# A boot stage rearranged: two products to GpSimd, the states' last sums to ScalarE, own scores ahead of the updates

## The chip, the cores and the metric

One core of a Trainium2 chip runs the whole kernel. The metric is device time in microseconds, as the median of several runs. The core has five engines with a queue each: TensorE (PE; its weight loads are PEld), VectorE (DVE), ScalarE (ACT), GpSimd (POOL) and SyncE (SP), which here only issues transfers. GpSimd does not read TensorE's result memory, PSUM, in this kernel; VectorE and ScalarE do.

## The reference

A recurrent attention block with a decaying state, and behind it a dense block with a shrinking activation:

```python
for t in range(S):                       # B, H, S, D = 4, 8, 768, 48
    cur = einsum('bhd,bhe->bhde', u * k[t], v[t])
    y[t] = einsum('bhd,bhde->bhe', r[t], state + cur)
    state = w[t][..., None] * state + einsum('bhd,bhe->bhde', k[t], v[t])
x = y as (B*S, H*D) = (3072, 384)
h = x @ w_in                             # 384 -> 2048
out = (h - tanh(h)) @ w_out              # 2048 -> 384
```

All in float32, with decays w between 0.80 and 0.95.

## The kernel before, in words

The sequence of each batch element is cut into two halves of 384 tokens, which makes eight blocks. The attention of a block is turned into matrix products over chunks of 64 tokens. Products of decays within each chunk come from scans on VectorE: `post` (from a token to the end of its chunk, method `behind`) and `pre` (from the chunk's start, divided by the chunk's whole decay, method `before`). `times_behind` multiplies k into `post`, `times_before` multiplies r into `pre`. Two sets of scores follow on TensorE: `own` (k·u with r, of which the diagonal is kept) and `earlier` (`post` with `pre`, of which what lies above the diagonal is kept). Masked copies on VectorE (`copy_predicated`) bring them into one tile, `scores`. The result of a block is the scores times v (`from_scores`) plus `pre` times the state at the start of each chunk (`from_states`).

While one block's dense products run on TensorE, the next block's attention is fitted in between them. The first block has nothing to hide behind: function `boot` does its attention alone, ahead of everything else, and this is the stage that the change touches. It handles the eight heads as four pairs, in two halves: `h1` is pairs 2 and 3, `h2` is pairs 0 and 1. For each half it runs, in this order of dependence: decays, `times_behind`, k times u on ScalarE (`times_u`), own scores, `post` transposed on TensorE (`turn_1`) and copied by ScalarE (`turn_2`), `times_before`, earlier scores, the products k·v for every chunk (`update_half`), and a scan over the chunks that turns them into states (`states_half`). `states_half` also returned one small sum for each pair, the state handed on to the next block. The results of a pair are copied from PSUM to the tiles `xT`, the input of the dense products (`result_out`). Pairs 0, 1 and 2 fill 96 of the 128 rows of xT[0], xT[1] and xT[2]; pair 3 goes to a tile `late`, from which six small transfers fill the holes, two for each xT tile (`fill_holes`).

At the same time the weights come in: sixteen tiles of 768 KB (`more_weights`, from SyncE's queue), each converted by three ScalarE instructions and one or two of VectorE (`convert`). There are five buffers for them. Six of the sixteen are issued in the boot; the second, third and fourth wait for a given matrix product on TensorE (`begin_behind`), those in the main loop for a ScalarE instruction.

The order on TensorE, VectorE, ScalarE and SyncE is the order in which the program is written, and each engine goes through its queue in order: an instruction that waits holds up all those behind it. Only GpSimd's order is left to the framework. Three PSUM tiles take turns in the boot (`scratch`), and the products k·v use two more (`pair`), which are later the first accumulators of the dense block.

## Time and profile before

| | us |
|---|---|
| median of 3 runs | 544.35 (544.01 to 544.61) |
| the profiled execution | 545.07 |
| its span, first to last instruction | 543.3 |
| PE busy | 534.1 (98%) |
| DVE busy | 459.0 (84%) |
| ACT busy | 403.7 (74%) |
| POOL busy | 6.5 (1%) |
| first dense product starts at | 23.50 |

Times in the trace count from the start of the span. A row of the timeline gives the start, the duration, the engine, the line of the kernel, the operation and its operands; the bracket tells how long the engine stood idle before it and what ended the wait. A row of the transfers gives the size of one and the time from its issue to its landing. The granted TensorE clock is 1.000 over the whole span.

### The profile page before, as it was taken

The page shows a single profiled execution, that of the slowest core. Times are in us where ns is not written, and L with a number is a line of the kernel's source. Part 1 is how long each engine was busy: PE and PEld are TensorE (multiplying, and loading weights), DVE is VectorE, ACT ScalarE, POOL GpSimd, SP SyncE. Part 2 cuts the span into 40 slices and gives each one's busy share as a digit, 9 for nine tenths or more (in the row PEclk, how much of TensorE's full clock was granted, in tenths as well). Part 3 has the DMA queues.
Part 4 walks back from the last instruction along what each step waited for, and adds up shares of the span by engine and source line. Part 5 has one row for each costly group of instructions (what it writes and reads, how often), then busy time and mean ns, then how long its engine had stood idle before and what let it go on. Part 6 is the DMA issues. An engine that isn't in the chain of part 4 may idle for free.

```text
span 543.3 us, 14866 instructions
## 1 busy us (share of the span) xinstructions
PE 534.1 (98%) x5682; PEld 403.3 (74%) x5682; DVE 459.0 (84%) x943; ACT 403.7 (74%) x814; POOL 6.5 (1%) x47
## 2 busy tenths in 40 slices
PE   7999999999999999999999999999999999999996
PEld 5756665678877777777887787877788788777874
DVE  7999999999989989798997979879797997557463
ACT  4899986888668876688767886688866885766561
POOL 1100000000000000000000000000000000000000
PEclk9999999999999999999999999999999999999999
DMA  7798732252311631154112532136321420100101
GB/s 276 234 402 311 259 119 74 97 137 63 122 42 54 162 118 57 43 147 119 60 56 87 122 103 70 48 97 151 84 89 46 122 27 3 56 1 0 45 1 46
DMA packets 53048, 56.34 MB, mean 104 GB/s; under 512 B 21488, under 2 KB 50928, under 8 KB 52976
## 3 DMA queue, kind: packets, MB, share of 16 engines
q1 hardware_dynamic: 52592, 55.18, 33.9%
q8 instruction: 48, 0.79, 0.6%
q14 instruction: 24, 0.20, 0.1%
q10 hardware_dynamic: 288, 0.10, 0.1%
q0 software_dynamic: 96, 0.07, 0.1%
HBM read 44.73 MB, written 4.72 MB: 91 GB/s over the span
## 4 chain that ended last, share of the span: by engine, by line
PE 88%; DVE 6%; ACT 2%; issue 2%; DMA 1%; SPq 0%; DVEq 0%
PE hp L871 41%; PE acc L999 27%; PE att L999 7%; PE att L757 4%; PE acc L950 3%; PE acc L977 2%; PE att L494 2%; PE att L575 1%; PE att L871 1%; ACT up L264 1%; DMA r<-in_rT 1%; DVE w_sb L268 1%; PE acc L871 1%; DVE scores L502 1%; DVE states L587 1%
## 5 line engine op out<-in xcount | busy, mean ns | idle before, releaser
L871 PE MATMUL hp<-xT,w_sb 128*128 128x384 f32 x738 | 259.3, 488 | 0.4 <-ACT h L876 0.4
L871 PEld LDWEIGHTS hp<-xT,w_sb 128*128 128x128 f32 x738 | 131.8, 190 | 70.0 <-ACT h L876 1.3
L999 PE MATMUL acc<-forms,g 128*128 128x128 f32 x954 | 133.2, 276 | 0.0
L876 ACT ACTIVATE h<-hp 128x384 f32<-128x384 f32 x123 | 60.3, 490 | 96.6 <-PE hp L871 96.5
L999 PEld LDWEIGHTS acc<-forms,g 128*128 128x128 f32 x954 | 122.0, 192 | 10.3
L879 DVE SCALAR_TENSOR_TENSOR h<-h,s 128x384 f32<-128x384 f32 x128 | 70.5, 551 | 51.9 <-ACT s L894 51.8
L920 DVE TENSOR_TENSOR g<-g 128x256 f32<-128x256 f32 x265 | 103.2, 418 | 7.4 <-PE acc L999 6.5
L895 ACT ACTIVATE qa<-s,shift 128x384 f32<-128x384 f32 x113 | 69.5, 615 | 3.7
L897 ACT ACTIVATE junk<-s,shift 128x384 bf16<-128x384 f32 x113 | 67.7, 599 | 0.0
L879 DVE SCALAR_TENSOR_TENSOR g<-qa,h 128x384 f32<-128x384 f32 x112 | 61.6, 550 | 1.6 <-ACT qa L905 0.2
L894 ACT ACTIVATE s<-h 128x384 f32<-128x384 f32 x113 | 59.2, 523 | 3.6
L999 PEld LDWEIGHTS acc<-w_sb,g 128*128 128x128 f32 x318 | 46.8, 191 | 9.7 <-ACT sums L967 0.3
L999 PE MATMUL acc<-w_sb,g 128*128 128x128 f32 x318 | 53.0, 276 | 0.0
L999 PE MATMUL att<-w_sb,g 128*128 128x128 f32 x212 | 35.5, 275 | 0.0
L999 PEld LDWEIGHTS att<-w_sb,g 128*128 128x128 f32 x212 | 31.1, 192 | 5.3
L1034 DVE TENSOR_TENSOR sums<-sums 128x256 f32<-128x256 f32 x84 | 32.8, 406 | 1.7 <-ACT sums L1011 1.4
L950 PE MATMUL acc<-w_sb,sums 128*128 128x384 f32 x96 | 33.9, 489 | 0.1
L264 ACT ACTIVATE up<-raw 128x768 f16<-128x768 f32 (+1 forms) x32 | 33.1, 1074 | 0.0
L950 PEld LDWEIGHTS acc<-w_sb,sums 128*128 128x128 f32 x96 | 17.9, 190 | 13.0 <-DVE sums L879 1.2
L417 DVE TENSOR_TENSOR_SCAN pre<-w,start 128x780 f32<-128x780 f32 x14 | 25.0, 1783 | 0.8
L429 DVE TENSOR_TENSOR_SCAN post<-w,seed 128x780 f32<-128x780 f32 x14 | 24.9, 1775 | 0.0
L897 ACT ACTIVATION_READ_ACCUMULATOR junk<-s,shift 128x1 f32 x113 | 21.1, 187 | 0.0
(118 smaller groups left out, 528.8 us busy)
## 6 DMA issues: line engine op xcount, KB each, us to landing
raw<-in_weights SPq DMA_DIRECT2D x16, 768.0 KB, 7.1
w<-in_wT SPq DMA_DIRECT2D x7, 780.0 KB, 4.7
k<-in_kT SPq DMA_DIRECT2D x7, 768.0 KB, 4.6
r<-in_rT SPq DMA_DIRECT2D x7, 768.0 KB, 4.6
v_sb<-in_v SPq DMA_DIRECT2D x8, 576.0 KB, 4.0
k<-in_tokens SPq DMA_DIRECT2D x7, 576.0 KB, 5.0
r<-in_tokens SPq DMA_DIRECT2D x7, 576.0 KB, 4.7
out_y<-sums SPq DMA_DIRECT2D x18, 128.0 KB, 1.8
```

The costliest lines, as they stand in the source:

```text
L264: return lambda: nc.scalar.activation(out=to, in_=of, func=AF.Copy, scale=scale, bias=bias)
L417: return nc.vector.tensor_tensor_scan(out=self.tile("pre")[:, cols], data0=self.tile("w")[:, cols], data1=start[:, 0:n * NCH * LP], initia ...
L871: nc.tensor.matmul(hp, lhsT=w_in_sb[:, f, kc, :], rhs=xT[kc], start=(kc == KC - 1), stop=(kc == 0))
L876: return h, nc.scalar.activation(out=h, in_=hp, func=AF.Copy, scale=1.0 / UPSCALE)
L879: return lambda: nc.vector.scalar_tensor_tensor(out=out, in0=in0, scalar=scalar, in1=in1, op0=op0, op1=ALU.mult)
L894: nc.scalar.activation(out=s, in_=h, func=AF.Square)
L895: nc.scalar.activation(out=qa, in_=s, func=AF.Square, bias=shift[:, 4:5])
L897: nc.scalar.activation(out=junk[:, 0:NB], in_=s, func=AF.Relu, bias=shift[:, 5:6], accum_out=excess[:, at:at + 1])
L920: return lambda: nc.vector.tensor_tensor(out=G[:, to:to + 2], in0=two(G, g_at(q, a0), g_at(q, a1)), in1=two(G, g_at(q, b0), g_at(q, b1)), ...
L950: nc.tensor.matmul(acc, lhsT=g[:, j * P:(j + 1) * P], rhs=w_out_sb[:, f, :], start=(f == self.first), stop=(f == NF - 1))
L999: nc.tensor.matmul(to, lhsT=G[:, g_at(q, a), :], rhs=rhs, start=start, stop=stop, skip_group_check=True)
L1034: ops.append(lambda op=op, at=at: nc.vector.tensor_tensor(out=at[0], in0=at[1], in1=at[2], op=OPS[op]))
```

## The change

`times_before` and `times_behind` can be given an engine, and for the second half both go to GpSimd; the second of them also moves up, ahead of VectorE's copy of the first half's scores. The small sums that followed the scans of the states are split. ScalarE copies one of their terms from PSUM into the next block's state tile (`last_half`, two copies for each half). One VectorE instruction for all four pairs adds the other term later, in the main loop (`onwards`, at step 3 of block 0). `earlier()` of the first half moves ahead of `turn_2` of the second. `from_states` no longer goes pair by pair in the boot. For the second half, own scores are computed ahead of `update_half`, and their masked copy stands ahead of the scans. The second weight load moves from behind the first `update_half` to behind the first `from_states`. The hole transfers of xT[2] and xT[1] all go to SyncE's queue and those of xT[0] to GpSimd's, where they alternated between the two. In the general path, which only runs for unusual decays, `together` copies by halves of rows.

```diff
+SPARE = 94
-        def times_before(self, p0, n):
+        def times_before(self, p0, n, engine=nc.vector):
             t = self.before_each(p0, n)
-            return nc.vector.tensor_tensor(...)
+            return engine.tensor_tensor(...)
-        def times_behind(self, p0, n):
+        def times_behind(self, p0, n, engine=nc.vector):
...
         def states_half(self, p0):
                 nc.vector.tensor_tensor_scan(out=to, data0=kv, data1=by, initial=0.0, op0=ALU.add, op1=ALU.mult)
-            return [lambda p=p0 + p, kv=kv: nc.vector.tensor_tensor(
-                out=states[1][:, p, 0, 0:D], in0=first_states[:, p, :, NCH - 1], in1=kv[:, :, 0], op=ALU.add)
-                for p, kv in enumerate(self.by_column)]
+        def last_half(self, p0):
+            for p, kv in enumerate(self.by_column):
+                nc.scalar.copy(out=states[1][:, p0 + p, 0, 0:D], in_=kv[:, :, 0])
+        def onwards(self, p0, n):
+            to = states[1][:, p0:p0 + n, 0, 0:D]
+            nc.vector.tensor_tensor(out=to, in0=first_states[:, p0:p0 + n, :, NCH - 1], in1=to, op=ALU.add)
...
-                      3: ("times_behind 2",),
+                      3: ("times_behind 2", "onwards"),
...
-        own = blk.own(ps, h1, spare=94, ahead=5, late=6)
+        own = blk.own(ps, h1, spare=SPARE, ahead=5, late=6)
         blk.turn_1(ps, h1)
         blk.times_before(h1, UP)
         earlier = blk.earlier(ps, h1)
         blk.behind(h2, UP)
         blk.take_whole(h2, UP)
+        blk.times_behind(h2, UP, nc.gpsimd)
         first_a, first_b = convert(*raws.pop(0), tiles=2)
         own()
         blk.turn_2(h1)
         blk.totals_by_column(h2)
         blk.update_half(pair, h1)
-        begin_behind(blk.done, more_weights(nc.sync))
-        blk.times_behind(h2, UP)
         blk.times_u(h2, UP)
         blk.turn_1(ps, h2)
+        earlier()
         blk.turn_2(h2)
-        earlier()
         blk.results(ps)
         blk.result("from_scores", both[0])
-        run(blk.states_half(h1))
-        blk.result("from_states", both[0], True, apart=True)
+        blk.states_half(h1)
+        blk.last_half(h1)
+        blk.result("from_states", both[0], True)
+        begin_behind(blk.done, more_weights(nc.sync))
         blk.before(h2, UP)
-        blk.update_half(pair, h2)
-        blk.times_before(h2, UP)
+        blk.times_before(h2, UP, nc.gpsimd)
         own = blk.own(ps, h2)
         own_scored = blk.done
+        blk.update_half(pair, h2)
         run(first_a[:1])
         blk.result_out((3,), [nc.scalar.copy] * 2)
         blk.result_out((2,))
         earlier = blk.earlier(ps, h2, ahead=1)
         scored = blk.done
-        onwards = blk.states_half(h2)
         own()
+        blk.states_half(h2)
         run(first_a[1:])
-        needed = 2 * KC - 2
-        blk.fill_holes([nc.sync, nc.gpsimd], range(needed, 2 * KC))
+        blk.last_half(h2)
+        blk.fill_holes(range(4, 6))
         begin_behind(own_scored, more_weights(nc.sync))
-        blk.fill_holes([nc.sync, nc.gpsimd], range(needed))
+        blk.fill_holes(range(2, 4))
+        blk.fill_holes(range(2), nc.gpsimd)
         begin_behind(scored, more_weights(nc.sync))
         later.load("w")
         second_a, second_b = convert(*raws.pop(0))
         third_a, third_b = convert(*raws.pop(0))
         run(second_a)
         more_weights(nc.sync)
         blk.results(ps)
         blk.yp.reverse()
-        blk.result("from_states", both[1], apart=True)
+        blk.result("from_states", both[1])
         earlier(1, 1)
         earlier(0, 1)
         for p in reversed(both[1]):
             blk.result("from_scores", (p,), True, more=True)
         later.load("k")
         more_weights(nc.sync)
-        run(onwards)
         run(first_b[:1])
         for p in reversed(both[1]):
             blk.result_out((p,), [nc.scalar.copy, nc.vector.tensor_copy])
```

More of the change, by code (lines that the diff above doesn't have):

```diff
@@ L769, in together, with fill_holes @@
                     stretch(of, cross)
-            self.result_out(ALL)
-            self.fill_holes([nc.sync])
-        def fill_holes(self, engines, which=range(2 * KC)):
+            self.result_out(ALL, None if spread else [nc.scalar.copy] * 2)
+            self.fill_holes()
+        def fill_holes(self, which=range(2 * KC), engine=nc.sync):
             for n in reversed(which):
@@ L776, in fill_holes @@
                 src = 64 * (n // KC) + 16 * (n % KC)
-                engines[n % len(engines)].dma_start(out=self.xT[i][64 * h + D:64 * h + 64],
-                                                    in_=self.late[src:src + 16, :])
+                engine.dma_start(out=self.xT[i][64 * h + D:64 * h + 64], in_=self.late[src:src + 16, :])
         def phase(self, ps, name):
@@ L1058, in plan @@
             phases = {6: ("turn",), 7: ("update",), 10: ("earlier",), 13: ("results",)}
-            before = {0: ("behind 2", "take_whole 2"), 2: ("behind 0", "take_whole 0"), 3: ("times_behind 2",),
+            before = {0: ("behind 2", "take_whole 2"), 2: ("behind 0", "take_whole 0"), 3: ("times_behind 2", "onwards"),
                       4: ("times_behind 0",), 5: ("before 2",), 6: ("before 0",), 7: ("times_before",),
```

6 lines of the change are left out of this document (3 added, 3 removed).

## The prediction

> **What bounds the kernel now.** I read the page first (TensorE is busy 98% of the span), then the windows of the trace by stage, because the change lies in the first 25 us only.
>
> ```profile
> 25.00:50.00 25.00, 24.62 (x84) 14.50 (x83) 22.76 (x42) 23.45 (x33) 0.00 (x0) 1.00 1.02 384
> 50.00:76.00 26.00, 26.00 (x247) 15.60 (x245) 25.35 (x48) 26.00 (x39) 0.13 (x2) 1.00 0.59 198
> 76.00:543.30 467.30, 462.24 (x4760) 357.37 (x4760) 390.18 (x819) 337.38 (x719) 2.21 (x25) 1.00 0.28 76
> ```
>
> The columns after the window's length are the busy times of PE, PEld, DVE, ACT and POOL, then the granted clock, the DMA engines' share and GB/s. From 76 us on TensorE alone is full, so a microsecond won or lost by then stays. Between 25 and 76 us three engines are full together, and the DMA engines up to 50 us: a gain at 25 us need not arrive at 76. Who leads there is told by the chain of waits, ScalarE's timeline, the issue of one weight load and the time from that issue to its landing.
>
> ```profile
> 50.47 0.56 DVE sums L879
> 76.10 2.20 PE acc L950 x6
> 36.59 0.92 ACT L264 ACTIVATE w_sb<-raw 128x768 f32<-128x768 f32 x1 [0.85 <-DMA raw<-in_weights]
> 22.81 0.69 SPq L251 DMA_DIRECT2D raw<-in_weights  x1
> raw<-in_weights SPq DMA_DIRECT2D x1, 768.0 KB, 13.8
> ```
>
> Back from 76.10 the chain is VectorE to 50.47, then ScalarE. ScalarE last stood idle at 36.59, 0.85 us for the sixth weight tile, which was issued at 22.81 and landed 13.8 us later, at 36.6. From there it works without a gap to 76 us. So the end follows the landing of these loads: a later landing goes through whole, while an earlier end of the boot would only lengthen the wait at 36.59.
>
> **The change part by part.** First the product k·decay of the second half, which GpSimd takes over and which stands earlier in the order.
>
> ```profile
> 3.88 0.68 SPq L369 DMA_DIRECT2D k<-in_kT  x1
> k<-in_kT SPq DMA_DIRECT2D x1, 384.0 KB, 8.4
> 12.36 0.96 DVE L443 TENSOR_TENSOR post<-k,post 128x768 f32<-128x768 f32 x1
> 0.82 0.20 POOL masks.py:197 MEMSET ident<- 128x128 f32 x1 [0.29 <-POOLq L1445]
> 0.96 0.75 POOL L171 MEMSET start<- 128x780 f32 x1
> 1.75 0.28 POOL masks.py:199 TENSOR_SCALAR_AFFINE_SELECT ident<-ident 128x128 f32<-128x128 f32 x1
> ```
>
> Its input k was issued at 3.88 and landed 8.4 us later, at 12.28. VectorE began at 12.36, so the earlier place cannot start it earlier: GpSimd begins at about 12.30. No row has a GpSimd product. From below it is 0.75 us, a write-only pass of 780 elements; from above 2.25 us, three such passes (two reads and a write that share nothing). The two MEMSETs give (0.75-0.20)/652 = 0.84 ns per element written and 0.09 us fixed; the select reads as well and takes 0.08 us more on 128 elements, 0.63 ns per element read. Two reads and a write of 768 elements: 768 x 2.10 + 0.09 = 1.70 us. This is the value I take. The product ends at 14.00, where VectorE's ended at 13.32.
>
> What waits for it is the transpose on TensorE, and its queue behind it.
>
> ```profile
> 10.35 0.88 PE L517 MATMUL att<-ident,post 128*128 128x128 f32 x6
> 11.16 0.93 PE L494 MATMUL att<-pre,post 48*64 48x64 f32 x48
> 13.38 0.87 PE L517 MATMUL att<-ident,post 128*128 128x128 f32 x6
> 14.31 0.90 PE L697 MATMUL att<-scores,v_sb 64*48 64x64 f32 x48
> 15.50 1.56 PE L679 MATMUL att<-pre,first_states 48*48 48x64 f32 x37 [0.28 <-PEq L717]
> 18.00 0.90 PE L494 MATMUL att<-r,k 48*64 48x64 f32 x48
> 13.24 1.02 DVE L502 COPY_PREDICATED scores<-mask_all,att 128x768 f32<-128x768 uint8 x1
> ```
>
> The transpose moves from 13.38 to 14.06 (+0.68). The products with the scores follow a transpose's start by 0.81 us (10.35 to 11.16): 14.87. VectorE no longer holds them, since its score copy of 13.24 now starts at 12.36, 0.88 earlier, and the scans behind it end before 15. The products with the states follow by 1.19 (14.31 to 15.50), drain included: 16.06. Without the split by pairs four places of the array alternate, as in the rows of 0.90 us; I take 0.90 for these 48 and end them at 16.96. The old form ran 15.50 to 17.16, so TensorE is by now 0.2 us ahead. Here begins the trouble: the second weight load, formerly behind the first half's update, now waits for this end.
>
> VectorE gains: the four small sums leave it (two of them in the way), and so does the product with r.
>
> ```profile
> 15.57 0.24 DVE L632 TENSOR_TENSOR states<-first_states,hp 128x48 f32<-128x48 f32 x1
> 17.95 0.96 DVE L436 TENSOR_TENSOR pre<-r,pre 128x768 f32<-128x768 f32 x1
> 18.83 0.75 DVE L631 TENSOR_TENSOR_SCAN first_states<-acc,first_totals 128x288 f32<-128x288 f32 x1
> 19.50 0.73 DVE L631 TENSOR_TENSOR_SCAN first_states<-hp,first_totals 128x288 f32<-128x288 f32 x1
> 16.82 0.25 PE L616 MATMUL acc<-v_sb,ks 64*64 64x48 f32 x1
> 22.68 0.89 PE L697 MATMUL att<-scores,v_sb 64*48 64x64 f32 x48 [0.24 <-DVE states L632]
> ```
>
> The input of the product with r, ready at 17.95 now, comes 0.88 and two sums (0.48) earlier, at 16.6, and GpSimd ends 1.70 later, at 18.3. TensorE does the own scores first, to 17.9 (16.96+0.90), then the update, to 19.0 (1.18, as from 16.82 to 18.00 now). Only then does it need that product, which is hidden with 0.7 us to spare, even at 2.25. Without this cover it would cost all it lasts beyond. VectorE's own scores are copied beside the update; its two scans (18.83 to 20.23, 1.40) follow it to 20.4, the states' products (0.90) to 21.3; the gap of 0.24 and the scores' products of 0.89 end at 22.4, where they now end at 23.57. That is about 1.15 us ahead on TensorE. The one sum for all pairs in the main loop, in place of the four, falls into a stretch in which VectorE was busy 22.76 of 25 us: nothing; without that room, 0.24 or a little more.
>
> ScalarE takes four copies. I price each like VectorE's 128x48 sum, 0.24.
>
> ```profile
> 15.18 0.91 ACT L264 ACTIVATE w_sb<-raw 128x768 f32<-128x768 f32 x1
> 16.62 0.97 ACT L729 COPY late<-att 48x384 f32<-48x384 f32 x2 [0.53 <-PE att L679]
> 17.99 2.01 ACT L264 ACTIVATE up<-raw 128x768 f16<-128x768 f32 x2
> 19.86 0.89 ACT L264 ACTIVATE w_sb<-raw 128x768 f32<-128x768 f32 x1
> 20.66 1.96 ACT L264 ACTIVATE up<-raw 128x768 f16<-128x768 f32 x2
> 23.29 0.84 ACT L729 COPY xT<-att 48x384 f32<-48x384 f32 x2 [0.67 <-PE att L697]
> 23.80 1.04 DVE L729 COPY xT<-att 48x384 f32<-48x384 f32 x2 [0.74 <-ACT xT L729]
> ```
>
> Its copy of the transposes moves with them, by 0.68. What followed at 15.18 so comes at 15.86: first two small copies (0.48), then the first conversion (0.91), to about 17.2. So the copies into the tile "late" go from 16.62 to 17.2 (+0.58), the next conversions from 17.99 to 18.57; these end at 20.58, and two more small copies at 21.0.
>
> SyncE's queue decides the rest.
>
> ```profile
> 18.12 0.64 SPq L777 DMA_DIRECT2D xT<-late  x1
> 18.95 0.41 SPq L251 DMA_DIRECT2D raw<-in_weights  x1
> 19.42 1.15 SPq L777 DMA_DIRECT2D xT<-late  x2
> raw<-in_weights SPq DMA_DIRECT2D x1, 768.0 KB, 4.3
> xT<-late SPq DMA_DIRECT2D x1, 24.0 KB, 4.5
> 25.21 0.30 PEld L871 LDWEIGHTS acc<-xT,w_sb 128*128 128x128 f32 x2 [0.50 <-DVE xT L729]
> ```
>
> The second load is issued at about 16.97, not at about 13.4 (its old trigger ends just before the transposes of 13.38), and lands 4.3 us later, at 21.27, where ScalarE has been ready since 21.0. Its three conversions take 2.76 (19.86 to 22.62) and end at 24.03, and ScalarE's halves of the last xT copies are queued behind them. VectorE's halves, which start 0.51 after ScalarE's (23.80 against 23.29), so start near 24.55 and end 1.04 later, at 25.6. So the 1.15 us on TensorE find no xT: the third part of the first dense product starts near 25.65, now 25.21.
>
> Both hole transfers for xT's last tile are now SyncE's; they start behind xT's copy, at 18.70 instead of 18.12, and take 0.64 and 0.58 (half of 1.15) to issue. The third load, free since 17.9, goes out at 19.9, not 18.95. The loads behind it follow in order, in a stream with no gap to catch up in: the sixth lands 0.95 us later, ScalarE waits for it until 37.5 and the chain passes it on. The holes of the second tile are queued behind the third load, at 20.3 and 20.9, and land 4.5 us later as their like did, at 25.4 at the latest of the two; this could make the 25.65 up to 0.4 more, still under 0.95. Those of the first tile go to GpSimd's queue behind its second product, 18.3, with seven microseconds to spare.
>
> **Sum.** 0.95 us on the profiled execution's 545.07 us (span 543.3) gives 546.0; that execution lies 0.72 above the median of 544.35, so on the median 545.3. With GpSimd at 0.75 the transposes are as early as now, and it is 0.0; at 2.25 it is 1.5. Small copies at 0.1 instead of 0.24 take off 0.3.
>
> **The rivals.** (a) Faster: the loads are early enough all the same, and TensorE's 1.15 us arrive: 543.2. It needs the second load down by 21.0 and the sixth no later than 1 us before 36.6. For it speaks that the old second load had its data 2.2 us before use (17.7 and 19.86); against it the wait of 0.85. It decides where the second load is issued before 16.6.
> (b) Slower: GpSimd is kept out while VectorE copies scores. Old scores, mask and PSUM data may amount to two reads of SBUF; then the copy of 12.36 to 13.38 holds the product until 13.40, 1.10 later, and 0.95 becomes 2.05: 546.4. No row shows both engines at work together on SBUF. The Trainium skill (SBUF — State Buffer, "Who interferes with whom") says that a VectorE instruction with two SBUF inputs shuts out a GpSimd instruction that reads SBUF for its whole length, and one with a single SBUF input does not; counted as mask and PSUM data, this copy has one, and by that rule the 0.95 stands.
> (c) It does nothing: the sixth load's landing hangs on the slowest DMA engine's backlog and not on the issue of the third, and the 0.44 at 25 us vanishes in ScalarE's wait: 544.4.
>
> **How the numbers follow.** About 0.2%, 1.09 us, is what a measurement can tell from no change here. The forecast has 0.60: its own range is 544.2 to 545.9, and somewhat less than half of it (0.27) lies above 545.44, because every unpriced wait adds; 0.33 lies within. Rival (a) 0.15, (b) 0.17, (c) 0.08. Faster 0.15, same 0.41, slower 0.44. The range from 543.2 to 546.8 takes in (a) and (b).
>
> **What would show it.** Right: GpSimd's first product starting at 12.3, not at 11.4, and lasting 1.4 to 2.0; the transposes near 14.06; the second load issued near 17.0; ScalarE idle before its conversion, with "DMA raw" as releaser; the third load issued near 19.9 and ScalarE's last wait ending near 37.5. Wrong: this wait ending at 36.6 or sooner, the first dense product starting before 23 with ScalarE's copies right behind, or a product of more than 2.5 us.

## The result, and the profile after

| | before | after |
|---|---|---|
| median, same chip (range) | 544.61 us (543.97 to 545.20) | 548.71 us (547.40 to 550.85) |
| ratio | | 1.0081, 95% interval 1.0061 to 1.0101 |
| profiled execution | 545.07 us | 548.48 us |
| its span | 543.3 us | 546.7 us |
| granted clock over the span | 1.000 | 0.998 |

The change makes the kernel 4.1 us slower. The forecast was 545.3, at most 546.8. The profiled execution is 3.41 us longer than the one of before. The chain of waits of after, first its start in the boot, then the place where the stage with three full engines ends:

```profile
17.19 5.38 DMA raw<-in_weights
22.59 0.94 ACT w_sb L265
23.53 1.85 ACT up L265 x2
25.73 1.03 DVE xT L736 x2
26.80 0.57 DVE w_sb L269
27.42 1.54 PE acc L877 x4
...
78.50 0.48 DVE sums L885
79.02 2.20 PE acc L956 x6
```

The accumulating product that started at 76.10 before starts at 79.02: 2.92 us of the 3.41 are there by then, and the chain goes back, with no ScalarE wait for a load after 25 us, to the dense product at 27.42 and to the second weight load. The same places in the timeline of after:

```profile
12.32 1.68 POOL L444 TENSOR_TENSOR post<-k,post 128x768 f32<-128x768 f32 x1 [9.12 <-DMA k<-in_kT]
16.92 1.68 POOL L437 TENSOR_TENSOR pre<-r,pre 128x768 f32<-128x768 f32 x1 [2.92 <-DVE pre L418]
17.20 0.97 ACT L736 COPY late<-att 48x384 f32<-48x384 f32 x2 [0.30 <-PE att L686]
17.19 0.34 SPq L252 DMA_DIRECT2D raw<-in_weights  x1
18.68 1.26 SPq L784 DMA_DIRECT2D xT<-late  x2
20.04 0.52 SPq L252 DMA_DIRECT2D raw<-in_weights  x1
20.61 1.14 SPq L784 DMA_DIRECT2D xT<-late  x2
22.59 0.94 ACT L265 ACTIVATE w_sb<-raw 128x768 f32<-128x768 f32 x1 [1.87 <-DMA raw<-in_weights]
25.73 1.03 DVE L736 COPY xT<-att 48x384 f32<-48x384 f32 x2 [2.88 <-ACT xT L736]
27.42 3.46 PE L877 MATMUL acc<-xT,w_sb 128*128 128x384 f32 x10 [3.13 <-DVE w_sb L269]
28.98 0.49 ACT L882 ACTIVATE h<-acc 128x384 f32<-128x384 f32 x1 [1.18 <-PE acc L877]
29.50 0.56 DVE L908 CUSTOM_DVE_ANT_0 s<-h 128x384 f32<-128x384 f32 x1 [1.19 <-ACT h L882]
```

and, in the timeline of before, the row that answers to the last one, with GpSimd's hole transfers:

```profile
17.39 1.57 POOL L777 DMA_DIRECT2D xT<-late  x3 [14.19 <-ACT late L729]
26.68 0.56 DVE L902 CUSTOM_DVE_ANT_0 s<-h 128x384 f32<-128x384 f32 x1 [0.30 <-ACT h L876]
```

The row `s<-h` is VectorE's first square of the hidden layer: it needs ScalarE's copy of the first dense product, which needs TensorE. It starts at 29.50 instead of 26.68, 2.82 us later. From there to the end of the stage VectorE is busy for 47.2 of 49.5 us in after and for 46.8 of 49.4 in before, so this start is the marker by which the experiments are read. The last output transfer is issued 2.92 us later (541.89 against 538.97). The remaining 0.48 us lie between that issue and the end of the span (4.81 us, before 4.33) and have nothing to do with the boot that I could find.

TensorE begins its first dense product early (two of twelve matrix products at 23.38) and then stands for 3.13 us: the next tile of xT is not complete. Two things are late in it. VectorE's copies into xT come behind ScalarE's, which stand behind the conversion of the second load; they start at 25.73 instead of 23.80, and the one into this tile is done by 26.3. Later still are the data in the tile's holes. The transfers into them, in the answer on DMA issues (name, queue, count, KB, us from issue to landing), issued in after from 20.5 to 22 us, and in before from 17 to 19 us:

```profile
xT<-late SPq DMA_DIRECT2D x2, 24.0 KB, 6.3
```

```profile
xT<-late POOLq DMA_DIRECT2D x3, 24.0 KB, 1.8
xT<-late SPq DMA_DIRECT2D x1, 24.0 KB, 2.0
```

The same 24 KB take 1.8 to 2.0 us in one kernel and 6.3 in the other. In before, four of the six are out ahead of the third load (18.95). In after, those of the tile that TensorE needs next are issued at 20.61, behind the third load (20.04) and with the second still on its way; they land at 27.1 and 27.3, the last thing to come before 27.42. The trace puts the end of the wait down to VectorE's conversion of 26.80, but in e10_third below the same products start ahead of that conversion (26.68 there). In that kernel these holes are not behind the third load while the second load is as late as here, and its timeline has

```profile
26.23 3.49 PE L877 MATMUL acc<-xT,w_sb 128*128 128x384 f32 x10 [1.36 <-DVE xT L736]
```

So of TensorE's late start the holes account for about 1.2 us, and the late load, by way of ScalarE's and VectorE's copies, for most of the rest.

What the second load lost by its new place is told by the windows from 14 to 18 us, before and after (columns as in the prediction; the last two are the share of time in which the DMA engines were busy, and GB/s):

```profile
14.00:18.00 4.00, 3.54 (x140) 3.07 (x141) 3.90 (x8) 3.40 (x7) 0.61 (x1) 1.00 0.60 205
```

```profile
14.00:18.00 4.00, 3.66 (x166) 3.39 (x166) 2.83 (x5) 3.63 (x8) 1.08 (x2) 1.00 0.02 7
```

In before the second load fills a stretch in which the DMA engines have nothing else to do; in after they stand idle there, and the load shares the time from 17.2 us on with the holes and the third load.

Part of the median has a second source. After's executions with a mean granted clock of 0.998 took 547.40 to 548.48 us, those with 0.993 to 0.996 took 548.71 to 550.85. A mean of 0.998 by itself says nothing of the boot: in the profiled execution of after the clock is 1.000 until 544 us and falls only in the last 2.3 us of the span. This is taken up with the experiments, because several of them show in the trace when the clock falls.

### The profile page after: what moved, and what is told of

Read it like the earlier page. It is cut to its first block, busy times and chain, and to the rows that moved or that the text cites. A ratio compares the mean times of both kernels' runs of the same rounds, so it can differ in the third digit from the quotient of the medians.

```text
span 546.7 us, 14865 instructions
## 1 busy us (share of the span) xinstructions
PE 532.7 (97%) x5682; PEld 402.0 (74%) x5682; DVE 457.1 (84%) x938; ACT 404.1 (74%) x818; POOL 9.4 (2%) x48
## 4 chain that ended last, share of the span: by engine, by line
PE 85%; DVE 7%; DMA 2%; issue 2%; ACT 1%; SPq 0%; POOL 0%; PEld 0%; PEldq 0%; DVEq 0%; POOLq 0%
PE hp L877 41%; PE acc L1005 26%; PE att L1005 6%; PE att L764 4%; PE acc L956 2%; PE acc L983 2%; PE att L495 2%; DVE w_sb L269 2%; DMA k<-in_kT 2%; PE att L576 1%; DMA raw<-in_weights 1%; DVE s L908 1%; DVE sums L885 1%; DVE h L885 1%; DVE states L588 1%
## 5 line engine op out<-in xcount | busy, mean ns | idle before, releaser
L1005 PEld LDWEIGHTS acc<-w_sb,g 128*128 128x128 f32 x318 | 46.8, 191 | 9.7 <-ACT sums L973 0.3
L956 PEld LDWEIGHTS acc<-w_sb,sums 128*128 128x128 f32 x96 | 17.9, 190 | 13.5 <-DVE sums L885 1.8
```

What stands on the lines that cost most here:

```text
L956: nc.tensor.matmul(acc, lhsT=g[:, j * P:(j + 1) * P], rhs=w_out_sb[:, f, :], start=(f == self.first), stop=(f == NF - 1))
L1005: nc.tensor.matmul(to, lhsT=G[:, g_at(q, a), :], rhs=rhs, start=start, stop=stop, skip_group_check=True)
```

## The experiments

Every kernel was run beside the kernel before. The table sorts them by the marker. "Late" is the start of ScalarE's copies into the tile `late`, "first square" that of VectorE's `s<-h`, "stage end" that of the product which stood at 76.10; these three are from the profiled execution. Time and ratio are of all runs, 4 to 10 for a kernel. The profiled executions of b1_load, e8_dve, e2_holes and e6_warm had a fallen clock in the boot, so their markers hold that as well. The kernel before had medians of 544.61 to 544.94 beside them.

| kernel | what it is | late | first square | stage end | median us | ratio (95%) |
|---|---|---|---|---|---|---|
| before | | 16.62 | 26.68 | 76.10 | 544.61 | 1 |
| b3_raw_first | before, sixth load ahead of k | 16.49 | 26.74 | 75.62 | 544.64 | 0.9996 (0.9976–1.0016) |
| r2_all_but_k | after, r's product, holes, second load back | 16.98 | 27.15 | 76.22 | 545.48 | 1.0014 (0.9996–1.0032) |
| f1_rest | r2, and k's product back | 16.95 | 27.26 | 76.32 | 545.20 | 1.0009 (0.9997–1.0021) |
| d1_delay | before, pure delay on ScalarE | 16.94 | 27.27 | 75.92 | 545.37 | 1.0011 (0.9998–1.0025) |
| b8_k | before, k's product on GpSimd | 17.31 | 27.48 | 76.47 | 545.28 | 1.0007 (0.9991–1.0023) |
| e3_both | after, holes and second load back | 17.77 | 28.16 | 77.65 | 547.02 | 1.0033 (1.0016–1.0050) |
| b7_r | before, r's product on GpSimd | 16.63 | 28.30 | 76.95 | 548.72 | 1.0071 (1.0051–1.0092) |
| b6_third | before, third load behind the holes | 17.37 | 28.45 | 77.09 | 545.74 | 1.0014 (0.9996–1.0033) |
| e1_load | after, second load back | 17.34 | 28.57 | 78.06 | 548.08 | 1.0058 (1.0040–1.0076) |
| e10_third | after, third load behind the holes | 17.60 | 28.64 | 79.25 | 548.69 | 1.0061 (1.0043–1.0080) |
| r1_holes_r | after, r's product and holes back | 17.46 | 28.82 | 77.89 | 548.30 | 1.0048 (1.0028–1.0069) |
| b4_pool | before, both products on GpSimd | 17.19 | 28.90 | 77.52 | 547.16 | 1.0038 (1.0021–1.0054) |
| e7_best | after, second load and k's product back, four holes on GpSimd | 17.68 | 29.30 | 78.34 | 547.62 | 1.0052 (1.0035–1.0069) |
| after | | 17.20 | 29.50 | 79.02 | 548.71 | 1.0081 (1.0061–1.0101) |
| e9_third_load | e1_load and e10_third together | 17.30 | 29.54 | 79.06 | 548.21 | 1.0054 (1.0036–1.0071) |
| e8_dve | after, k's product back | 17.45 | 29.78 | 79.77 | 548.80 | 1.0066 (1.0043–1.0089) |
| b1_load | before, second load late | 17.30 | 30.67 | 80.21 | 549.29 | 1.0074 (1.0051–1.0096) |
| e2_holes | after, holes back | 17.25 | 31.44 | 81.61 | 548.63 | 1.0063 (1.0042–1.0084) |
| e6_warm | after, eight idle products | 18.80 | 32.18 | 81.70 | 548.12 | 1.0044 (1.0027–1.0061) |

Stage end minus first square is 48.6 to 50.6 us in every row, over 5.5 us of the marker: what delays the first square is passed on to within about a microsecond, whatever delayed it. "Late" explains much less: d1, r2, f1 and after lie within 0.3 us of each other in it, and after is over 2.2 us later than the other three in the first square.

### The loads first: second load, holes, both

The first theory was that the late second load does it, the rival that the hole transfers do.

```diff
 # e1_load: after, with
+        begin_behind(blk.done, more_weights(nc.sync))   # behind update_half(h1), as before
...
-        begin_behind(blk.done, more_weights(nc.sync))   # behind from_states(h1)
 # e2_holes: after, with
+        blk.fill_holes(range(5, 6), nc.gpsimd)          # alternating, as before
+        blk.fill_holes(range(4, 5))
 # e3_both: both; b1_load: before, with the second load behind from_states(h1)
```

> The changed kernel, its second weight load moved back behind the first half's update. Theory L (the late second load holds ScalarE's queue and with it xT): the load is issued near 13.4 and lands near 18, ScalarE converts from 20.7 without the wait of 1.9 us, the last xT copies end near 25, the first dense product goes on near 25.5 instead of 27.4; 545.2 to 546.5. Theory P (GpSimd's product, which moves the transposes from 13.38 to 14.06, is what counts): nothing changes, 548 to 549. Theory H (the hole transfers of xT[1], both on SyncE behind the third load, are what counts): TensorE still waits for a landing near 27 us, 548.

> The changed kernel, its hole transfers alternating between SyncE and GpSimd as before the change. Theory L: ScalarE still waits to 22.6 for the second load and xT is still late; the first dense product goes on near 26.4 instead of 27.4; 547.2 to 548.2. Theory H: the product goes on near 25, 545 to 546. Theory P: 548 to 549.

> Both: the second load moved back and the hole transfers alternating. Theory L with H: first dense product going on near 24.5 to 25, 544 to 545.3. Theory L alone: as with the load alone. Theory P: 548 to 549.

> The kernel before, with only the second weight load moved behind the first half's states products (which end near 17.2). Theory L: the load lands at 21.5 to 22.6, ScalarE waits for it 1.7 to 2.7 us, and the kernel is slower by 1.5 to 3 us: 546 to 547.6. Theories P and H: no change, 544.3 to 544.9.

Neither alone brings the time back (548.08 and 548.63), and both together only a good part (547.02). Yet the late load alone, put into the kernel before, costs as much as the whole change: 549.29, a ratio of 1.0074 against 1.0081, and more than the 546 to 547.6 expected. So the load is enough by itself, but is not alone: in e1_load, where it is early, TensorE goes on only at 26.48, when the holes issued behind the third load have landed (5.0 and 5.4 us). What the load does is in ScalarE's timeline of b1_load:

```profile
24.21 0.89 ACT L264 ACTIVATE w_sb<-raw 128x768 f32<-128x768 f32 x1 [3.52 <-DMA raw<-in_weights]
```

and in the DMA issues of that kernel from 17 to 18 and 18 to 22 us:

```profile
raw<-in_weights SPq DMA_DIRECT2D x1, 768.0 KB, 6.3
...
xT<-late POOLq DMA_DIRECT2D x3, 24.0 KB, 5.4
xT<-late SPq DMA_DIRECT2D x3, 24.0 KB, 6.1
```

It lands 6.3 us after its issue, not 4.3, ScalarE's halves of xT stand behind its conversion, and all six hole transfers, which are issued behind it, become slow, on GpSimd's queue too. TensorE's last wait there (to 27.91) ends with VectorE's copies, though, not with the holes, which were all there by 27.1.

### One product alone

What is left when load and holes are as before? First both products on GpSimd in the kernel before, then after with k's product back on VectorE, alone and with more undone.

```diff
 # b4_pool: before, with
-        blk.times_behind(h2, UP)
+        blk.times_behind(h2, UP, nc.gpsimd)             # at its place in before, behind update_half(h1)
...
+        earlier()                                       # ahead of turn_2(h2), as in after
         blk.turn_2(h2)
-        earlier()
...
-        blk.times_before(h2, UP)
+        blk.times_before(h2, UP, nc.gpsimd)
 # e8_dve: after, with
-        blk.times_behind(h2, UP, nc.gpsimd)
+        blk.times_behind(h2, UP)                        # behind update_half(h1)
 # e7_best: e8_dve and e1_load, and
-        blk.fill_holes(range(2, 4))
-        blk.fill_holes(range(2), nc.gpsimd)
+        blk.fill_holes(range(4), nc.gpsimd)
```

> The kernel before, with only the two products given to GpSimd. Theory P: the first ends at 14.0 to 14.6 instead of 13.3, the copy into late and with it the third load come 0.7 to 1.2 us later, and the kernel is slower by 0.5 to 1.5 us: 545.1 to 546.1. If VectorE's relief of 1.9 us outweighs it: 543.5 to 544.3.

> The changed kernel with only the product k times decay back on VectorE at its old place. Theory P: transposes at 13.4, the second load issued near 16.4 instead of 17.2, the third near 19.1; everything 0.7 to 1 us earlier, and fewer runs with a fallen clock: 546.8 to 548. If the product counts for nothing: 548.7.

> The changed kernel with three things undone: the second load back behind the first update, the product k times decay back on VectorE, and the four holes of xT[1] and xT[0] on GpSimd's queue, where they do not stand behind the third load. If the late load, the late product and the holes are all there is: transposes at 13.4, first dense product going on at 24 to 24.5, 543.5 to 544.8. If ScalarE's small copies, the pairs kept together or the own scores ahead of the update cost something of their own: 545 or more.

The two products cost 2.2 us in the kernel before (547.16 against 544.94; expected were 0.5 to 1.5), and taking k's product back out of after brings nothing (548.80). e7_best, meant as the best of both, came to 547.62: its first square is at 29.30, since r's product runs on GpSimd until 20.2 and four hole transfers stand behind it. So it had to be the other one, or the copies into `late` coming 0.57 us later than in before (b4_pool). Three kernels and the rest of the change tell these apart:

```diff
 # b8_k: b4_pool with times_before(h2, UP) on VectorE    # k's product alone
 # b7_r: b4_pool with times_behind(h2, UP) on VectorE    # r's product alone; both keep earlier() moved
 # d1_delay: before, with
         run(first_a[:1])
+        for _ in range(2):
+            nc.scalar.copy(out=idle[:, 0:480], in_=blk.tokens("r", h1, UP)[:, 0:480])
         blk.result_out((3,), [nc.scalar.copy] * 2)
 # f1_rest: e3_both with both products on VectorE
```

> Kernel before, with one thing added: two ScalarE copies of 480 elements into a tile that nobody reads, just ahead of ScalarE's copies into late, which so come 0.5 to 0.7 us later (at about 17.2, as in after). Theory F (a delay there passes on as it is): both ends that set VectorE's first square of the hidden layer, TensorE's first product and ScalarE's third conversion, move by the same 0.5 to 0.7, and the time is 545.1 to 545.6. Theory A (the delay grows, because the hole transfers then fall behind load data): 546.5 or more. Rival N (hidden in ScalarE's idle 0.67 and 0.26 us): within 0.3 of the kernel before.

> Kernel before, with one of the two products alone on GpSimd, the one of k with the decay (with earlier() ahead of the transposes behind it). It takes 1.68 us from 12.3 where VectorE's took 0.96 from 12.36, so the copies into late come at 17.2 instead of 16.62. Theory F: the time is 0.5 to 0.8 above the kernel before, 545.1 to 545.6. Theory A: as with both products on GpSimd, 546.8 to 547.5.

> Kernel before, with the other product alone on GpSimd, the one of r with the decay. It runs at about 17.9 to 19.6 and the three hole transfers that GpSimd issues stand behind it in its queue, at 19.0 or later instead of 17.39, behind the third load (issued 18.95). Theory G (GpSimd's queue: the product holds the holes up, and they land behind the load's data): the first dense product goes on at 25.5 or later and the time is 545.8 to 547.3. Rival (the product leaves VectorE's path, which has 0.96 us less to do): 543.6 to 544.6.

> Kernel after with both products back on VectorE, the second load and the hole transfers where the kernel before has them: what is left of the change are the states' last sums by ScalarE copies, the pairs' scans kept together, and the own scores ahead of the update. Theory: these parts carry nothing of the loss; VectorE's first square stays within 0.5 of 26.7 and the time is 544.0 to 545.2. Rival (they delay the chain, as ScalarE's four copies and the later update do): 546 or more.

k's product, a pure delay at the same place, and all the rest of the change (ScalarE's copies, the pairs together, own scores ahead) cost 0.4 to 0.6 us each, and none of the three intervals excludes zero. The delay does not grow much: theory F of d1_delay holds, although its copies into `late` came only 0.32 us later, not the 0.5 to 0.7 intended, and the first square 0.59. f1_rest's first square is 0.58 us late, just outside the 0.5 expected. r's product alone costs 3.95 us, more than the 545.8 to 547.3 expected and more than both products in b4_pool; at full clock the two kernels are alike (545.80 and 546.07 here, 545.44 to 546.44 there), but 8 of 10 executions of b7_r had a lower mean clock, against 5 of 9, which is taken up below. By its own length the product adds 0.41 us (VectorE's last copies into xT start at 24.21 instead of 23.80). The rest comes from its place in GpSimd's queue, ahead of three hole transfers. GpSimd's timeline, the DMA issues from 18 to 22 us and VectorE's first square in b7_r:

```profile
18.07 1.70 POOL L436 TENSOR_TENSOR pre<-r,pre 128x768 f32<-128x768 f32 x1 [14.87 <-DVE pre L417]
19.70 1.63 POOL L777 DMA_DIRECT2D xT<-late  x3
28.30 0.56 DVE L902 CUSTOM_DVE_ANT_0 s<-h 128x384 f32<-128x384 f32 x1 [1.51 <-ACT h L876]
```

```profile
xT<-late SPq DMA_DIRECT2D x3, 24.0 KB, 4.8
xT<-late POOLq DMA_DIRECT2D x3, 24.0 KB, 4.8
```

and the same transfers in b8_k, where GpSimd was free for them at 18.09, and the marker in b8_k:

```profile
xT<-late POOLq DMA_DIRECT2D x3, 24.0 KB, 1.7
```

```profile
18.09 1.64 POOL L777 DMA_DIRECT2D xT<-late  x3 [3.94 <-ACT late L729]
27.48 0.56 DVE L902 CUSTOM_DVE_ANT_0 s<-h 128x384 f32<-128x384 f32 x1 [0.86 <-ACT h L876]
```

In b7_r the transfers are issued 2.31 us later than in before (19.70 against 17.39), behind the third load (18.96), and each takes 4.8 us instead of 1.8. The last lands at 25.5, and TensorE begins its first dense product at 25.57. In b8_k they leave at 18.09, ahead of the third load (19.65), and take 1.7. That is the mechanism by which a product that nobody waits for costs microseconds.

### Both causes in one square

If the late load and r's product are two causes of which each is enough, then after without the one and with the other must stay slow, and without both be fast. The hole transfers are shared by both queues in all four.

```diff
 # r1_holes_r: e2_holes with times_before(h2, UP) on VectorE
 # r2_all_but_k: e3_both with times_before(h2, UP) on VectorE
```

> Kernel after with r's product back on VectorE and the hole transfers shared by SyncE and GpSimd as before; the second load stays late and k's product stays on GpSimd. Theory D (two causes, each enough by itself: the late second load, and GpSimd's queue held by r's product): the load alone still costs most of the loss, ScalarE waits over 1 us for it, and the time is 547 to 549.5. Rival (the holes alone did it): 545 to 546.

> The same with the second load back at its old place too: of the change stay k's product on GpSimd, ScalarE's four copies, the pairs kept together and the own scores ahead. Theory D: nothing of the two causes is left; what remains is the later copy into late (17.2 to 17.4), passed on as it is, and the time is 545.2 to 546. Rival: 546.5 or more, as with both products on GpSimd and the same loads and holes (547.02).

| median us | r's product on VectorE | on GpSimd |
|---|---|---|
| second load as before | 545.48 (r2_all_but_k) | 547.02 (e3_both) |
| second load late | 548.30 (r1_holes_r) | 548.63 (e2_holes) |

Both expectations of theory D hold (548.30 and 545.48), and the load is enough by itself here too. Together the two cost little more than the load alone: both hold up the first dense product, and the one that comes last sets its start. The load does so by way of ScalarE's queue. In r1_holes_r ScalarE waits for it, and TensorE goes on when VectorE's copies into xT, behind ScalarE's, are there; these rows and VectorE's first squares of r1_holes_r and r2_all_but_k show how much later this makes it:

```profile
23.00 0.90 ACT L265 ACTIVATE w_sb<-raw 128x768 f32<-128x768 f32 x1 [2.02 <-DMA raw<-in_weights]
26.71 3.49 PE L877 MATMUL acc<-xT,w_sb 128*128 128x384 f32 x10 [1.93 <-DVE xT L736]
28.82 0.56 DVE L908 CUSTOM_DVE_ANT_0 s<-h 128x384 f32<-128x384 f32 x1
```

```profile
27.15 0.56 DVE L908 CUSTOM_DVE_ANT_0 s<-h 128x384 f32<-128x384 f32 x1 [1.03 <-ACT h L882]
```

For r's product the square shows less. With the second load as before the kernel that has it lies 2.4 us above before and 1.5 above the kernel without it; the intervals of the two ratios overlap, and the mechanism of b7_r is not seen: in e3_both GpSimd's holes leave from 18.55 on, ahead of the third load (20.00), and the DMA issues from 18.9 to 20.2 us have

```profile
xT<-late POOLq DMA_DIRECT2D x3, 24.0 KB, 1.7
```

Its second-half k landed 0.8 us later than that of r2_all_but_k (12.7 against 11.9), which by itself makes for later copies into `late` in that execution (17.77 against 16.98). What r's product costs there, and how, stays open.

### Let the third load wait instead

If load data ahead of the holes are the trouble, the third load can go out behind all of them.

```diff
-        begin_behind(own_scored, more_weights(nc.sync))
         blk.fill_holes(...)                             # xT[1], xT[0]
+        begin_behind(own_scored, more_weights(nc.sync))
 # b6_third: in before; e10_third: in after; e9_third_load: in e1_load
```

> Kernel before, with one edit: the third weight load is issued behind all six transfers into the holes of xT instead of between the second and the third pair of them. Theory Q (a 24 KB hole transfer lands only after the 768 KB load data that went out ahead of it, whichever engine issued it): SyncE's two late holes, which took 4.5 to 5.1 us behind the third load, now land within 2.5 us of their issue, TensorE's first dense product is held by the VectorE copies alone and goes on by 24.9 at the latest, and the time is 543.9 to 544.7. Rival T (the load is what counts; one us less of lead moves the loads behind it): holes faster all the same, but the conversions behind the third load come later and the time is 545 to 546.

> Kernel after, with one edit: the third weight load is issued behind all six hole transfers. Theory Q: only the late second load is still in flight beside the holes, which land at 23 to 24 instead of 27.1 to 27.4; then ScalarE's copies behind the conversion of that load set the start, the first dense product goes on at 25.3 to 26.3 instead of 27.42, and the time is 546.2 to 547.3. Rival C (the copies into the late tile come too late, the loads have nothing to do with it): at 27 as before this edit, 548.1 to 549.

> Kernel after, with two edits: the second weight load back at its old place (behind the first update), the third one behind all six hole transfers. Theory Q: no load data stand ahead of the holes, they land within 2.5 us, by 23.2; the first dense product goes on when the last copies into xT are done, 24.9 to 25.3, and the time is 544.7 to 545.6. Rival P (the GpSimd product itself, begun at 12.3, makes the boot's chain late whatever the loads do): 25.8 or later, 546 or more. Without the third load moved, the second alone back gave 548.08.

The holes did what theory Q said: in e9_third_load the transfers take 1.8 to 1.9 us, and TensorE goes on with its dense product at 24.46. And yet the time stays at 548.21, nowhere near the expected 544.7 to 545.6. The timeline of e9_third_load (TensorE, SyncE, ScalarE, VectorE) shows what is late instead:

```profile
24.46 3.49 PE L877 MATMUL acc<-xT,w_sb 128*128 128x384 f32 x10 [0.17 <-DVE xT L736]
21.41 1.76 SPq L252 DMA_DIRECT2D raw<-in_weights  x2
27.31 0.91 ACT L265 ACTIVATE w_sb<-raw 128x768 f32<-128x768 f32 x1 [3.13 <-DMA raw<-in_weights]
29.54 0.56 DVE L908 CUSTOM_DVE_ANT_0 s<-h 128x384 f32<-128x384 f32 x1 [3.12 <-ACT h L882]
```

The third load now goes out at 21.41 and ScalarE waits 3.13 us to convert it. ScalarE's copy of the first hidden tile stands behind that conversion in its queue, so the first square starts at 29.54, as late as in after. Theory Q was right about the transfers and wrong about the time, and rival P, that GpSimd's product makes the chain late, is wrong too. The first square has two suppliers, TensorE with the holes and ScalarE with the third load, and SyncE's queue gives one of them the first place. e10_third keeps the late second load: TensorE goes on at 26.23, as theory Q had it, ScalarE waits for four loads in turn (1.37, 0.44, 0.23 and 1.20 us), and the time does not move (548.69). b6_third pays the same way, less: its first dense product starts at 24.26, ScalarE waits 1.32 us for the load, and the median is 545.74, above theory Q's range and in rival T's, though its interval still holds no change.

### Does the stage follow the sixth load?

```diff
 # b3_raw_first: before, with
+        more_weights(nc.sync)
         later.load("k")
-        more_weights(nc.sync)
```

> Kernel before, with one edit: the sixth weight load is issued ahead of the next block's k instead of behind it. If the stage from 25 to 76 us follows that load's landing (the prediction's claim), it ends earlier by what the load gains, 0.5 to 1 us, and the time is 543.4 to 544.2. If it follows the end of the boot (the first dense product), the time stays within 0.3 of the kernel before, or rises where the later k makes the next block wait.

ScalarE's last wait for a load in the stage shrinks from 0.85 to 0.27 us, in the timeline of b3_raw_first:

```profile
31.68 0.92 ACT L264 ACTIVATE w_sb<-raw 128x768 f32<-128x768 f32 x1 [0.27 <-DMA raw<-in_weights]
```

The stage ends 0.48 us earlier in this one execution (75.62), and the median is the same (544.64 against 544.66). So by this trace the load's wait was worth at most half a microsecond (the interval of the ratio alone would allow a gain of up to 1.3 us), and the end of the stage follows VectorE's first square.

### The granted clock

> The changed kernel with eight idle matrix products on TensorE at the end of the boot (into a PSUM tile that is free there), which fill about 2 us of the 3 to 4 us in which it waits for xT. Nothing else is earlier. Theory C (in some runs the wait is long enough for the granted clock to fall to 0.5 for some 7 us, which adds 1.5 to 3 us): the clock stays at 1 through the boot in every run, the slow half of the runs (548.7 to 550.9) is gone, the median falls by about 1 us to 547.3 to 547.9. Without C: no change, 548.7, or slower by what the products hold up.

e6_warm puts eight products that nobody needs (`busy(pair[0], 8)`) into TensorE's queue ahead of its wait, to keep the clock up there. The time is 548.12, not clearly different from after's, and in its profiled execution the clock fell already at 15.3 us, ahead of the eight products; it settles nothing. What the clock does is seen in other kernels. Windows of 2 us in e2_holes, where TensorE stood from 22.91 to 26.70 (columns as in the prediction; the granted clock is the third from the end):

```profile
24.00:26.00 2.00, 0.00 (x0) 0.00 (x0) 0.73 (x2) 2.00 (x5) 0.00 (x0) 0.90 0.95 317
28.00:30.00 2.00, 2.00 (x4) 1.01 (x3) 0.00 (x0) 0.00 (x0) 0.00 (x0) 0.50 1.02 408
30.00:32.00 2.00, 2.00 (x5) 1.06 (x4) 0.56 (x2) 1.09 (x2) 0.00 (x0) 0.50 1.07 390
32.00:34.00 2.00, 2.00 (x7) 1.24 (x6) 1.43 (x3) 1.45 (x3) 0.00 (x0) 0.90 1.05 407
```

While TensorE stands, the clock drops to half, and stays there until it has worked for several microseconds: four or five matrix products in a window instead of seven. In after's profiled execution, with 3.13 us of idleness, it did not drop. In two others it dropped after shorter waits; their rows of TensorE, and windows of the time just behind, first b1_load, then e8_dve:

```profile
27.91 5.18 PE L871 MATMUL acc<-xT,w_sb 128*128 128x384 f32 x10 [2.17 <-DVE xT L729]
28.70:32.10 3.40, 3.40 (x7) 1.89 (x6) 2.22 (x6) 2.65 (x4) 0.00 (x0) 0.50 1.04 396
```

```profile
27.10 5.16 PE L877 MATMUL acc<-xT,w_sb 128*128 128x384 f32 x10 [2.95 <-DMA xT<-late]
28.00:30.00 2.00, 2.00 (x4) 1.07 (x4) 0.46 (x3) 1.07 (x3) 0.00 (x0) 0.50 1.07 415
```

The Trainium skill (TensorE: Matmul & The Clock Gate, Part 1) gives a free-running window of about 3.4 us, after which an idle array gets half the clock. The length of the drop agrees with such a window: it is 3.41 us in b1_load and e8_dve and 6.83, twice that, in e2_holes. The length of the wait does not: 2.17 and 2.95 us had the drop and 3.13 had none. So these traces do not show what sets it off; a window that runs free would say why the same kernel has it in some executions only.

The spread goes with the clock. In b7_r the two executions with a mean clock of 1.000 and 0.998 took 545.80 and 546.07 us, and the eight with 0.992 to 0.997 took 548.28 to 551.26. The first square of its profiled execution (546.07) is 1.62 us late, and its time is 1.3 above the kernel before: at full clock the wait costs about what it lasts. The remaining 2.7 us of its median go with the lower clock; that is argued from the recorded clocks, since no slower execution of b7_r or of after has a trace. The size fits: by an estimate from the drops above, half the clock for 3.41 or 6.83 us costs TensorE 1.7 or 3.4 us. In r1_holes_r it is the same, 546.31 to 546.84 at 0.999 or more, 548.30 and more below.

## Why the prediction was wrong

- **GpSimd's first product.** Right: 12.32 and 1.68 us, forecast 12.30 and 1.70. The price put together from two MEMSETs and a select held to 0.02 us. The transposes start at 14.06, as forecast, and cost 0.58 us at the copies into `late` (17.20, as forecast).
- **Rival (b), GpSimd shut out by VectorE's score copy.** Refuted: the product took 1.68 us beside two such copies, as r's product did in e3_both (1.69 us from 16.89), where VectorE stood still until 18.55. The rule of the Trainium skill told there (SBUF — State Buffer, "Who interferes with whom") agrees with these rows.
- **ScalarE's four copies.** 0.20 us each, forecast 0.24. Right in kind.
- **The second load.** Its issue was right (17.19, forecast 16.97). Its landing was mis-sized: 5.38 us instead of 4.3 in after, 6.31 in b1_load. I took the time from the row of before, and there the load had the DMA engines nearly to itself. ScalarE so waited 1.87 us, not 0.3, and VectorE's last copies into xT started at 25.73, not 24.55. This is the first of the two steps that failed.
- **The holes of the second tile.** This is the step that failed by most: "land 4.5 us later as their like did, at 25.4 at the latest". They were issued at 20.61, 0.3 later than forecast, and took 6.3 us, so the last landed at 27.3 and TensorE went on at 27.42. "Their like" had been issued behind one load; these stood behind two.
- **"The end follows the landing of these loads ... an earlier end of the boot would only lengthen the wait at 36.59".** Wrong, and the error that hid the other two. I put down 0.95 us for the loads and let the 0.44 us (at most 0.85) of the holes and copies vanish under it. b3_raw_first shows the sixth load worth at most 0.48 us, and the table that the first square is passed on nearly whole. The third load did go out near 19.9 as forecast (20.04), but ScalarE's last wait, which was to end near 37.5, is gone in after: ScalarE was already later than the loads. With the right marker the same two misjudged landings would have stood in the sum.
- **r's product "is hidden with 0.7 us to spare".** True of the product and beside the point: GpSimd's queue was counted for the holes of the first tile only. b7_r shows what a hold-up of that queue does: 3.95 us of median, 1.3 of them at full clock. In after the change moves the holes of the second tile off that queue, and they lose their place to the third load on SyncE's instead.
- **TensorE's 1.15 us ahead.** Nearly gone before they could be used: a pause of 0.89 us in `earlier`, which the trace calls issue and gives no releaser, let the scores' products end at 23.45 instead of 22.4. Seven kernels with the new order have the pause, of 0.3 to 0.9 us; e2_holes and e3_both have none of over 0.25, and d1_delay, in the old order, has one of 0.46. Its cause stays open.
- **The clock.** Not foreseen. By the recorded clocks it is about a quarter of after's loss: 547.62 is the middle one of the three executions at 0.998, 548.71 the median of all.
- **Rivals (a) and (c)** fell with the sign. (a) needed the second load issued before 16.6, which was not so; (c) let everything vanish in ScalarE's wait, which is no longer there.

No kernel here beats the one before. What is harmless of the change, f1_rest, gains nothing either (545.20 against 544.77).

## What to carry to other kernels

A transfer's time from issue to landing belongs to the traffic around it, so a row of it may be carried over only to a place with the same loads in flight; ask of each small transfer that is moved which large one is now ahead of it, and of each large one which idle stretch of the DMA engines it leaves. An engine that issues transfers has a queue like the others: work put on an idle GpSimd delays what it issues behind it, even if nobody waits for the work. And before anything is hidden in a wait, test which start the stage really follows: here one row (VectorE's first square) told the end of the stage to about a microsecond in twenty kernels, while the wait that looked like the bound was worth half a microsecond.

## What the runs showed of the hardware

- A transfer of 24 KB within SBUF took 1.7 to 2.4 us when no 768 KB load was in flight at its issue (3.1 and 3.5 us in two cases, each less than a microsecond ahead of a load), and 3.1 to 6.6 us when one was, on SyncE's queue and on GpSimd's alike. Most of those landed right behind the load: in after the second load landed at 22.6 and the four transfers issued behind it at 22.7 to 23.2. The Trainium skill (DMA: Bandwidth & Descriptors, "Issuing engines are not separate DMA queues") says that transfers of all issuing engines run on the same DMA engines and interleave there; the runs agree in that GpSimd's queue was no way around a load. The Trainium skill (the same page, "Queues, rings and completion order") has each DMA engine take turns between queues packet by packet. If a load is several packets to each of them, that would let GpSimd's transfers pass SyncE's load, and in b7_r they did not (4.8 us, landing 0.4 to 1.3 us behind the load).
- GpSimd's product of two 128x768 float32 operands took 1.67 to 1.70 us in every run, with or without VectorE at work, against 0.93 to 0.96 on VectorE.
- The second load, 768 KB, took 4.2 to 6.3 us from issue to landing in the boot, 4.2 to 4.6 where it went out near 13.5 us and 4.7 to 6.3 from 17.2 us on. What it shares its time with (holes, the next load) differs; how much each takes was not measured.
- The second half's inputs landed up to a microsecond apart from run to run: its k at 11.9 us in r2_all_but_k and at 13.0 in e7_best. In b6_third its decays came 0.77 us after VectorE was ready, in before without a wait. Single profiles in the table above carry this scatter in "late" and "first square"; the medians don't rest on it.
